# Gated linear attention followed by a rational feed-forward: explicit activation-table loads, the state's decay folded into an exp, and a new order of steps

## The chip, the cores and the metric

The kernel runs on one core of a Trainium2 chip. The metric is the device time in microseconds (us) of one execution; lower is better. Each time given is the median over several executions of the same program. The engines are called PE (matrix products; PEld is its weight load), DVE (vector), ACT (scalar: exp, ln, reciprocal, casts), POOL (GpSimd) and SP (which only issues transfers).

## The reference

Two stages, in float32. The first is a recurrent attention with a forget gate for each key channel, over 4 batches, 8 heads, 768 tokens and head size 48:

```python
f = 1.0 / (1.0 + np.exp(-f_logit))
for t in range(S):
    state = f[:, :, t, :, None] * state + np.einsum('bhd,bhe->bhde', k[:, :, t], v[:, :, t])
    y[:, :, t] = np.einsum('bhd,bhde->bhe', q[:, :, t], state)
```

The second takes the 3072 rows of 384 values that come out of it through a feed-forward of width 2048 with a rational function in the middle:

```python
h = x @ w_in
P = a[0] + a[1] * h + a[2] * h2 + a[3] * h3          # h2 = h*h, h3 = h2*h
Q = 1.0 + np.abs(b[0]) * np.abs(h) + np.abs(b[1]) * h2
out = (P / (Q + 1e-06)) @ w_out
```

## The kernel before

**Units.** The work is cut into 12 units of 256 tokens of one batch: unit n is chunk n // 4 of batch n % 4, so units 0 to 3 have no state to wait for, and unit n needs the state that unit n-4 left. A unit holds two chunks of 128 tokens. All steps of a unit are short functions, and their order, over all units, is written out in the string ORDER (lines 19 to 95): each entry is a step's name, the unit, and its further arguments; `@0` to `@3` names one of four PSUM slots (two banks each) that the step opens. Every engine executes its instructions in exactly that order, so a step that waits holds up all later steps of its engine. Semaphore waits between the engines follow from the data.

**Attention steps of a unit.** `ld` (SP queue for f, k and q, POOL queue for v) loads. `ef` (line 280) is exp(-f), `ls` (line 285) ln(1 + that), both on ACT. `cs` (lines 295 and 300) makes, on PE, the running sums of the logarithms over the tokens with triangular matrices, and with 2 further columns for each pair of heads the sum over a whole chunk, the logarithm of the state's decay. `A` (line 308, ACT) is exp of the running sums, once with scale 1 (x = 1, for k) and once with -1 (x = 0, for q). `ae` (line 444, ACT) is exp of the chunk sums, in two instructions of 64 partitions each, which put the two heads of a pair into the two halves of a small tile whose other halves stay zero. `xa` (line 313, DVE, or POOL with the mark p) multiplies k or q by A. `T` transposes both on PE, `Te` copies them out of PSUM (ACT with the mark s, else DVE), `sc` makes the scores, `mk` (line 358, DVE) masks them, `vm` (POOL) packs v, `yb` and `yi` make the output y, `ic` and `si` the new state, `st` (line 449, DVE) multiplies it by the decay `ae`, and `ye` copies y out of PSUM as x.

**Feed-forward steps.** `h` (line 460) is x @ w_in on PE, four blocks of 128 features in a step; `hy` (line 472) casts them out of PSUM on ACT. The square is `sq` (DVE) or `sa` (line 481, ACT); `ab` is the absolute value (DVE); their sum is `zv` (DVE) or `zd` (line 494, an accumulating transfer issued by POOL). `rq` (line 499) is the reciprocal of the denominator on ACT. The numerator is `p1`, `p2`, `pm` on DVE and a sum by `tv` (line 527, DVE) or `ta` (line 523, an accumulating transfer issued by POOL); `gm` (line 531, DVE) multiplies both. `o` (line 540) is the product with w_out on PE, `oe` (line 548 on ACT with the mark s, else DVE) copies it out, and `so` stores it. Numbers behind a step's unit name the range of 16 feature blocks: `8 16` is a half (2048 elements per partition), `0 16` the whole (4096).

**Activation tables.** ACT evaluates exp, ln and reciprocal from a table set that has to be active. Exp and ln have a common set, reciprocal is in another one. The kernel names the common set once, at its start (line 135); all later loads are placed by the compiler ahead of the instructions that need them. In the trace they stand under the line of the instruction that they serve.

Of the kernel before, what the change touches and what calls it, by code (L numbers as in the profile page):

```python
# [8 lines left out]
F32 = mybir.dt.float32  # L9
BF16 = mybir.dt.bfloat16  # L10
# [12 lines left out]
wi 0 8 16; cz 1; ae 0 2 4; A 0 0 0 2; ls 1; xa 0 0 0 2; xa 0 1 2 4; xa 0 1 0 2; ld 1 q; T 0 2 4 @2; cs 1 @3  # L23
Te 0 2 4 s; fr; ic 0 @1; ae 1; st 0 0; A 1 1; si 0 1; T 0 0 2 @0; xa 1 1 0 4 p; st 0 1; sc 0 1 @2; Te 0 0 2 s
mk 0 1; ld 2 q; A 1 0; wi 2 8 16; ic 1 @1; sc 0 0 @0; ef 3; ld 2 k; wi 1 8 16; st 1 0; fb; ls 2; wi 3 8 16
mk 0 0; ls 3; xa 1 0 0 4 p; cs 2 @3; yb 0 2 4 @2; ae 2; yi 0 1; ld 4 f; vm 1; A 2 0; T 1 @0; wi 2 0 8; A 2 1
yb 0 0 2; wi 3 0 8; Te 1; si 1 1; xa 2 0 0 4 p; ye 0; sc 1 1 @3; sc 1 0 @0; h 0 12 16 @2; mk 1 0; wi 0 0 8
wi 1 0 8; st 1 1; h 0 8 12 @0; ld 2 v; hy 0 12 16; mk 1 1; ld 3 k; yi 1 1 @1; hy 0 8 12; yb 1 0 2; cs 3 @2
xa 2 1; A 3 0; p1 0 8 16; T 2 @3; A 3 1; sq 0 8 16; yb 1 2 4; h 0 4 8 @0; ye 1 s; ab 0 8 16; Te 2 s; pm 0 8 16
h 0 0 4 @1; ld 5 f; ae 3; hy 0 4 8; zv 0 8 16; sc 2 0 @3; hy 0 0 4; h 1 0 4 @2; mk 2 0; ld 3 q; vm 2; ef 4  # L30
ld 3 v; ic 2 @0; p2 0 8 16; hy 1 0 4; h 1 4 8 @1; ld 4 k; sq 0 0 8; ls 4; sc 2 1 @3; hy 1 4 8; h 1 12 16 @2
ab 0 0 8; mk 2 1; xa 3 1 0 4 p; ld 6 f; ef 5; hy 1 12 16; st 2 0; yb 2 2 4 @1; yb 2 0 2; ls 5; xa 3 0; yi 2 1
si 2 1; cs 4 @3; ye 2 s; p1 1 0 8; ld 4 q; sa 1 0 8; h 2 0 4 @2; p1 0 0 8; ab 1 0 8; ld 7 f; T 3 @1; st 2 1
vm 3; ld 4 v; hy 2 0 4; zv 0 0 8; h 1 8 12 @0; ld 5 k; Te 3 s; tv 0 8 16; A 4 1; h 2 4 8 @2; pm 0 0 8; ld 8 f
hy 1 8 12; ic 3 @1; A 4 0; xa 4 1 0 4 p; sc 3 1 @0; st 3 0; ae 4; mk 3 1; ef 6; si 3 1; cs 5 @3; ef 7; st 3 1
xa 4 0 0 4 p; sc 3 0 @0; ld 5 q; hy 2 4 8; h 2 8 12 @1; mk 3 0; ls 6; ld 6 q; ld 5 v; ab 1 8 16; h 2 12 16 @2
ae 5; A 5 0; p1 1 8 16; A 5 1; ld 6 k; yb 3 0 2 @0; p2 1 0 8; hy 2 12 16; yb 3 2 4; p2 0 0 8; yi 3 1; T 4 @3
hy 2 8 12; ye 3; xa 5 0 0 4 p; ls 7; Te 4; ld 7 q; ta 0 0 8; pm 1 0 8; sc 4 0 @2; si 4 0 @1; ic 4; rq 0 0 16
sc 4 1 @0; p1 2 8 16; cs 6 @3; ta 1 0 8; zv 1 0 8; wo 0 4; st 4 0; vm 4; mk 4 1; xa 5 1 0 4 p; si 4 1; st 4 1
h 3 12 16 @0; mk 4 0; vm 5; A 6 1; wo 8 12; si 5 0 @1; gm 0 0 8; ic 5; ae 6; ef 8; wo 12 16; h 3 8 12 @2  # L40
A 6 0; wo 4 8; st 5 0; ab 2 8 16; hy 3 12 16; ld 6 v; yb 4 2 4 @3; sq 1 8 16; yi 4 0; hy 3 8 12; h 3 4 8 @0
xa 6 1; sa 2 8 16; yb 4 0 2; pm 1 8 16; h 3 0 4 @2; ld 7 v; hy 3 4 8; gm 0 8 16; si 5 1; yi 4 1; ls 8; T 5 @0
ab 2 0 8; hy 3 0 4; st 5 1; p1 2 0 8; o 0 1 0 4 @1; Te 5 s; sq 2 0 8; cs 7 @2; ye 4 s; sa 3 0 8; p2 2 8 16
h 4 4 8 @0; p2 1 8 16; xa 6 0; o 0 0 0 4; ae 7; ta 1 8 16; hy 4 4 8; h 4 0 4 @3; zv 1 8 16; zd 2 0 8; A 7 1
sc 5 1 @0; pm 2 0 8; A 7 0; o 0 0 12 16; o 0 1 12 16; mk 5 1; xa 7 0 0 4 p; sc 5 0 @2; o 0 1 4 8; rq 1 0 16
mk 5 0; yb 5 2 4 @0; o 0 0 4 8; ld 10 q; pm 2 8 16; ld 7 k; o 0 1 8 12; o 0 0 8 12; zv 2 8 16; T 6 @2
hy 4 0 4; p1 3 0 8; yi 5 0; yi 5 1; yb 5 0 2; gm 1 0 8; oe 0 0 2 s; h 4 12 16 @3; Te 6 s; so 0 0 2; gm 1 8 16
h 4 8 12 @1; ye 5 s; sq 3 8 16; hy 4 12 16; o 1 0 12 16 @2; ld 9 f; hy 4 8 12; ab 3 0 8; si 6 0 @0; ic 6
tv 2 8 16; sc 6 1 @3; rq 2 0 16; o 1 1 12 16; zd 3 0 8; sc 6 0 @1; ab 3 8 16; o 1 0 0 4; mk 6 1; o 1 0 8 12
xa 7 1 0 4 p; o 1 0 4 8; mk 6 0; o 1 1 0 4; sa 4 0 16; zd 3 8 16; o 1 1 4 8; p2 2 0 8; st 6 0; vm 6; tv 2 0 8  # L50
yb 6 2 4 @3; yb 6 0 2; o 1 1 8 12; p1 3 8 16; ld 9 v; yi 6 1; yi 6 0; gm 2 8 16; h 5 0 4 @1; oe 1 0 2 s
ye 6 s; so 1 0 2; pm 3 0 8; T 7 @2; hy 5 0 4; si 6 1; ld 10 f; p2 3 0 16; h 5 12 16 @3; Te 7 s; ld 8 q
rq 3 0 8; p1 4 0 8; o 2 0 12 16 @1; h 5 4 8 @2; gm 2 0 8; rq 3 8 16; st 6 1; vm 7; o 2 0 8 12; ld 8 v
pm 3 8 16; ld 9 k; cs 8 @0; hy 5 12 16; ab 4 8 16; o 2 1 0 4; ld 11 f; tv 3 0 8; hy 5 4 8; sc 7 1 @3
o 2 1 8 12; p1 4 8 16; o 2 1 12 16; ab 4 0 8; sc 7 0 @2; o 2 1 4 8; A 8 0; pm 4 0 8; o 2 0 4 8; ef 9; ld 8 k
mk 7 1; xa 8 0 0 4 p; o 2 0 0 4; A 8 1; ef 10; mk 7 0; ld 9 q; yi 7 0 @3; ae 8; ta 3 8 16; oe 2 0 2 s
si 7 0 @0; p2 4 0 8; h 6 0 4 @2; sa 5 0 8; p1 5 0 8; yb 7 0 2; pm 4 8 16; ic 7; ls 9; yb 7 2 4; h 5 8 12 @1
p2 4 8 16; hy 6 0 4; st 7 0; ta 4 8 16; ls 10; tv 4 0 8; yi 7 1; si 7 1; h 6 4 8 @2; hy 5 8 12; zd 4 0 8
# [24 lines left out]
o 7 0 12 16; p1 10 0 8; o 7 1 8 12; tv 9 8 16; o 7 0 8 12; sa 10 0 8; yb 11 0 2; gm 8 8 16; h 10 12 16 @2
ye 11 s; pm 9 0 8; o 7 1 12 16; zd 10 0 8; hy 10 12 16; h 11 4 8 @1; pm 10 0 8; ta 9 0 8; hy 10 8 12
# [19 lines left out]
def kernel(  # L104
# [12 lines left out]
    nc = tc.nc  # L117
# [492 lines left out]
```

## Time and profile before

| | |
|---|---|
| median of 3 runs | 237.73 us (235.79 to 239.01) |
| profiled execution, its time | 236.52 us |
| profiled execution, its span on the core | 234.8 us |
| PE busy | 197.0 us, 2868 matrix products |
| DVE busy | 195.4 us |
| ACT busy | 200.4 us, of it 16 table loads |
| POOL busy | 84.3 us |
| read and written in HBM | 25.17 MB and 4.72 MB |

The span is the profiled execution alone, from its first to its last recorded event; the time of that execution is 1.7 us longer. Busy times are unions of an engine's instructions. Three engines are busy for 83 to 85% of the span, so no share by itself says which of them sets the time; that is read stage by stage.

### The profile page before, as it was taken

How to read it: one execution, taken by the hardware profiler on the slowest of the kernel's cores; microseconds unless marked ns; L12 is line 12 of the kernel's file. 1: busy time of each engine (PE TensorE's matmuls, PEld its weight loads, DVE VectorE, ACT ScalarE, POOL GpSimd, SP SyncE). 2: the span in 40 equal slices, each digit the busy share in tenths (PEclk: the TensorE clock that was granted, in tenths of full speed). 3: DMA queues.
4: the chain of work that ended last, by engine and by line, in shares of the span. 5: the costliest groups of instructions: out<-in, count | busy, mean ns of one | idle time of the engine just before them, and what ended most of it. 6: DMA issues, size and time to landing. Idle time of an engine off the chain costs nothing.

```text
span 234.8 us, 6576 instructions
## 1 busy us (share of the span) xinstructions
PE 197.0 (84%) x2868; PEld 140.4 (60%) x2868; DVE 195.4 (83%) x225; ACT 200.4 (85%) x208; POOL 84.3 (36%) x95
## 2 busy tenths in 40 slices
PE   0246998999499789999888399998999999999972
PEld 0234676787357557667466366856766776867540
DVE  3147696999999969999998817999998999999970
ACT  2657347999989999999999999799899999999841
POOL 5207902508584141460341160170746431212000
PEclk9998599999859999999999979999999999999999
DMA  6999999795799986789989994489799999979723
GB/s 145 246 228 259 226 210 204 108 254 127 123 159 147 178 159 159 175 148 219 265 169 198 261 225 40 92 172 178 150 197 199 210 202 190 194 162 207 163 67 67
DMA packets 61388, 41.58 MB, mean 177 GB/s; under 512 B 51376, under 2 KB 56496, under 8 KB 61360
## 3 DMA queue, kind: packets, MB, share of 16 engines
q0 software_dynamic: 20096, 22.29, 58.8%
q1 hardware_dynamic: 40976, 18.88, 34.7%
q8 instruction: 22, 0.36, 0.6%
q14 instruction: 6, 0.05, 0.1%
q10 hardware_dynamic: 288, 0.00, 0.1%
HBM read 25.17 MB, written 4.72 MB: 127 GB/s over the span
## 4 chain that ended last, share of the span: by engine, by line
PE 34%; ACT 29%; DVE 24%; issue 8%; DMA 2%; SPq 1%; DVEq 0%; ACTq 0%
PE hp L460 11%; PE op L540 9%; ACT hy L472 7%; ACT qi L499 5%; DVE scm L358 4%; DVE hy L514 4%; PE y L371 3%; ACT A L308 3%; ACT h L481 3%; DVE g L531 3%; PE cs L295 3%; PE tp L327 3%; DVE g L519 2%; DMA f<-in_f_logit_dram 2%; PE sc L350 2%
## 5 line engine op out<-in xcount | busy, mean ns | idle before, releaser
L460 PE MATMUL hp<-x,w_in_sb 128*128 128x256 bf16 x576 | 70.4, 275 | 6.3 <-ACT ae L444 3.5
L540 PE MATMUL op<-w_out_sb,g 128*128 128x384 bf16 x384 | 70.5, 329 | 2.0 <-DVE g L531 1.8
L460 PEld LDWEIGHTS <-w_in_sb 128*128 128x128 bf16 x576 | 55.3, 98 | 17.9 <-issue 8.7
L472 ACT CAST hy<-hp 128x1024 bf16<-128x1024 f32 x48 | 47.6, 1016 | 7.9 <-PE hp L460 7.6
L540 PEld LDWEIGHTS <-g 128*128 128x128 bf16 x384 | 35.7, 98 | 25.0 <-DVE g L531 2.8
L499 ACT ACTIVATE qi<-z 128x2048 bf16<-128x2048 bf16 (+1 forms) x20 | 45.0, 2258 | 0.1
L494 POOL DMA_DIRECT2D z<-h x17 | 17.6, 1074 | 47.3 <-DVE z L485 15.1
L358 DVE TENSOR_TENSOR scm<-sc,mask 128x1024 bf16<-128x1024 f32 x24 | 28.8, 1218 | 4.6 <-PE sc L350 4.5
L531 DVE TENSOR_TENSOR g<-g,qi 128x2048 bf16<-128x2048 bf16 (+1 forms) x22 | 28.9, 1316 | 0.9 <-ACT qi L499 0.7
L519 DVE TENSOR_TENSOR g<-g,h 128x2048 bf16<-128x2048 bf16 x24 | 29.2, 1225 | 0.0
L481 ACT ACTIVATE h<-hy 128x2048 bf16<-128x2048 bf16 (+1 forms) x13 | 26.5, 2048 | 0.0
L523 POOL DMA_DIRECT2D g<-hy x15 | 13.8, 922 | 31.3 <-DVE hy L514 18.9
L514 DVE TENSOR_SCALAR hy<-hy,a_sb 128x2048 bf16<-128x2048 bf16 (+1 forms) x23 | 22.5, 987 | 0.2
L295 PE MATMUL cs<-lsp,Ui 128*128 128x384 bf16 (+1 forms) x39 | 12.1, 374 | 11.1 <-ACT lsp L285 10.5
L308 ACT ACTIVATE A<-cs 128x768 f32<-128x768 f32 (+1 forms) x26 | 19.1, 763 | 2.2 <-PE cs L300 2.0
L313 POOL TENSOR_TENSOR qkp<-q,A 128x768 bf16<-128x768 f32 x8 | 15.4, 1927 | 15.6 <-ACT A L308 14.0
L449 DVE TENSOR_TENSOR state<-sv,ae 128x384 bf16<-128x384 f32 x20 | 11.0, 551 | 10.2 <-PE sv L426 6.7
L313 POOL TENSOR_TENSOR qkp<-k,A 128x768 bf16<-128x768 f32 x7 | 14.3, 2045 | 14.2 <-ACT A L308 14.2
L509 DVE TENSOR_SCALAR g<-hy,a_sb 128x2048 bf16<-128x2048 bf16 (+1 forms) x21 | 18.5, 883 | 0.5 <-ACT hy L472 0.3
L327 PE MATMUL tp<-ident,qkp 128*128 128x128 bf16 x192 | 14.1, 231 | 5.2 <-DVE qkp L313 4.0
L485 DVE TENSOR_SCALAR z<-hy 128x2048 uint16<-128x2048 uint16 (+1 forms) x22 | 17.4, 792 | 0.2 <-ACT hy L472 0.2
L327 PEld LDWEIGHTS <-qkp 128*128 128x128 bf16 x192 | 12.4, 104 | 6.9 <-DVE qkp L313 4.1
(71 smaller groups left out, 267.2 us busy)
## 6 DMA issues: line engine op xcount, KB each, us to landing
z<-h POOLq DMA_DIRECT2D x17, 512.0 KB, 6.7
g<-hy POOLq DMA_DIRECT2D x15, 512.0 KB, 5.5
f<-in_f_logit_dram SPq DMA_DIRECT2D x11, 384.0 KB, 6.0
k<-in_k_dram SPq DMA_DIRECT2D x11, 384.0 KB, 6.8
q<-in_q_dram SPq DMA_DIRECT2D x11, 384.0 KB, 7.1
out_dram<-osb SPq DMA_DIRECT2D x22, 192.0 KB, 3.8
v<-in_v_dram POOLq DMA_DIRECT2D x12, 192.0 KB, 6.8
w_in_sb<-in_moe_w_in_dram POOLq DMA_DIRECT2D x8, 192.0 KB, 6.9
```

What stands on the lines that cost most here:

```text
L308: nc.scalar.activation(t, src, AF.Exp, scale=1.0 if x else -1.0)
L313: i = (nc.gpsimd if eng == "p" else nc.vector).tensor_mul(s["qk"][:, x, :, hh, 0:D], s["qk"[x]][:, hh].rearrange("p h i d -> p i h d"), s[ ...
L327: nc.tensor.transpose(t[:, x, i, p, :], s["qk"][:, x, i, 2 * p:2 * p + 2, :].rearrange("t h d -> t (h d)"), ident)
L358: return nc.vector.tensor_mul(t, s["sc", g].rearrange("s r a i t -> s (r a) (i t)"), mb)
L460: nc.tensor.matmul(t[:, m - m0, :].rearrange("f (j t) -> f j t", j=UB), w_in_sb[:, kk, m * P:(m + 1) * P], s["x"][:, :, kk, :], start=(kk ...
L472: nc.scalar.copy(fl(big(s, "hy"), m0, m1), fl(s["hp", m0], 0, m1 - m0))
L481: return nc.scalar.activation(fl(big(s, "h2"), m0, m1), fl(big(s, "hy"), m0, m1), AF.Square)
L499: return nc.scalar.add_instruction(mybir.InstActivation(name=nc.get_next_instruction_name(), func=AF.Reciprocal, ins=[nc.scalar.lower_ap(f ...
L514: return nc.vector.tensor_scalar(fl(big(s, "hy"), m0, m1), fl(big(s, "hy"), m0, m1), a_sb[:, 1:2], a_sb[:, 0:1], op0=ALU.mult, op1=ALU.add)
L519: return nc.vector.tensor_mul(fl(big(s, "g"), m0, m1), fl(big(s, "g"), m0, m1), fl(big(s, "h2"), m0, m1))
L531: return nc.vector.tensor_mul(fl(big(s, "g"), m0, m1), fl(big(s, "g"), m0, m1), fl(big(s, "qi"), m0, m1))
L540: nc.tensor.matmul(s["op", g][:, j, 0:DM], big(s, "g")[:, m, C * j:C * j + C], w_out_sb[:, m, :], start=(s["on", j] == 1), stop=(s["on", j ...
```

## The change

Five edits. (1) A new step `tab` puts a table load with a named set into ACT's order: `tab 1` ahead of a run of reciprocals, `tab 0` ahead of a run of exp and ln. (2) The step `ae` and its tiles go. `cs` places the chunk sums as 8 columns behind the first (and second) running sum, 4 columns for each of two pairs of heads in each bank, and adds 1e4 to those of the wrong half with a product of the identity and a constant `hsel`; `A` with x = 0 takes these 8 columns along in the same exp, where exp(-1e4) gives the zeros; `st` reads its decay from the tile of `A`. (3) The tiles of `A` get a second buffer and 16 more columns. (4) ORDER is a new order of all steps. In it reciprocals, and exp and ln, stand in longer runs (seven `tab` steps in all), unit 1's `ld f` stands ahead of unit 0's, and `ef 1`, `ls 1`, `cs 1` and `A 1` ahead of most of unit 0's. (5) In the new ORDER some steps are on another engine or take another width: two `tv` and one `zv` of a half become `ta` and `zd`; one `sq` of a half goes to ACT, where the `sa` steps cover two wholes and eleven halves instead of one and twelve; `ye` of units 0 and 3 and `Te` of units 1 and 4 go to ACT, `ye` of unit 8 and `Te` of units 8, 10 and one half of unit 0 to DVE; the evacuations `oe` of units 0 and 2 and of the last half of unit 11 go to DVE, that of unit 5 to ACT; some `p1` are split into halves and some `p2`, `pm` and `gm` joined to wholes. A step `dm` is defined and not used.

The ACT instructions between the first and the third `tab` in the new order, in the program as built, are: reciprocals, casts and copies behind `tab 1`; then, from the last cast of unit 4 to the first of unit 5, one `ye`, `tab 0`, `ls 7`, `ef 8`, `Te 6`, `ef 9`, `A 7 0`, `ls 8`, `A 7 1`, `ls 9`, a whole `sa 3`, `tab 1`, a whole `rq 2` and one `ye`.

```diff
 ORDER = """
-ab_ b a; ci; ld 0 f 0 2; ld 0 k 2 4; cu 1; ld 0 f 2 4; ld 1 f; cu 0; ld 0 v; ld 2 f; cm; fa; ld 0 q 2 4
-ef 0 2 4; ef 0 0 2; ab_ a a; cz 3; cz 0; ld 0 q 0 2; cz 2; ef 1; ls 0 2 4; ls 0 0 2; ld 0 k 0 2; cs 0 0 2 @0
-cs 0 2 4 @1; ld 1 k; A 0 1 0 2; vm 0; A 0 0 2 4; ld 1 v; ld 3 f; A 0 1 2 4; xa 0 0 2 4; ae 0 0 2; ef 2
...
-mk 0 0; ls 3; xa 1 0 0 4 p; cs 2 @3; yb 0 2 4 @2; ae 2; yi 0 1; ld 4 f; vm 1; A 2 0; T 1 @0; wi 2 0 8; A 2 1
-yb 0 0 2; wi 3 0 8; Te 1; si 1 1; xa 2 0 0 4 p; ye 0; sc 1 1 @3; sc 1 0 @0; h 0 12 16 @2; mk 1 0; wi 0 0 8
...
+ab_ a a; cz 3; cu 0; ld 1 f; ab_ b a; ld 0 f 2 4; cu 1; ci; cm; cz 0; wi 0 8 16; ld 2 f; ld 0 f 0 2
+ld 0 k 0 2; cz 2; ld 0 v; ld 0 k 2 4; fa; ef 0 2 4; ef 1; ld 0 q 0 2; ld 0 q 2 4; cz 1; ls 1; cs 1 @0
+ef 0 0 2; ls 0 2 4; ld 1 k; A 1 0; cs 0 2 4 @1; ef 2; ls 0 0 2; A 1 1; cs 0 0 2 @2; vm 0; ld 3 f; ld 1 v
...
+cs 2 @1; ls 3; xa 1 0 0 4 p; sc 0 0 @3; A 2 0; si 1 1; mk 0 0; A 2 1; ld 2 v; st 1 1; fr; T 1 @3; ld 4 f
+wi 2 0 8; yb 0 0 2; Te 1 s; wi 1 0 8; cs 3 @1; ld 5 f; xa 2 1 0 4 p; ye 0 s; sc 1 1 @2; A 3 0; yi 1 1 @3
+mk 1 1; h 0 8 12 @0; A 3 1; vm 1; wi 0 0 8; xa 2 0; sc 1 0 @2; hy 0 8 12; wi 3 0 8; h 0 12 16 @1; mk 1 0
...
+ld 8 f; ta 1 0 8; tab 1; rq 0 8 16; yi 4 0; tv 0 0 8; yb 4 2 4; si 5 1; h 3 12 16 @1; p2 1 8 16; ld 7 v
...
+o 0 1 4 8; p1 2 8 16; tab 0; ls 7; ic 6; p2 2 0 16; ld 9 q; o 0 1 0 4; ef 8; cs 7 @2; Te 6 s; pm 2 0 16
...
 """
-    ind = consts.tile([P, UB], BF16, name="ind")
+    ind = consts.tile([P, UB, 2], BF16, name="ind")
+    hsel = consts.tile([P, UB, 2, 2], BF16, name="hsel")
-    rings("A", 1, [2, 2, DM], F32)
+    rings("A", 2, [2, 2, DM + 16], F32)
-    rings("ae", 2, [HP, UB, 2], F32)
-            for t in ring["ae"]:
-                nc.vector.memset(t.rearrange("p a j r -> p (a j r)"), 0.0)
+            nc.vector.memset(hsel, 0.0)
+            for r in range(2):
+                nc.vector.memset(hsel[E * r:E * r + E, :, :, 1 - r], 1.0e4)
+    def tab(i):
+        nc.scalar.preload_act_table_set(("natural_log_exp_and_others", "reciprocal_and_small")[i])
@@ def cs
-        s["al", a0] = t[:, 0, 448:448 + UB * (a1 - a0)].rearrange("p (a j) -> p a j", j=UB)
+        w0 = nh * D
+        for i in range(2):
+            nc.tensor.matmul(t[:, i, w0:w0 + 8], ident, hsel.rearrange("p j w r -> p (j w r)"),
+                             start=False, stop=True, skip_group_check=True)
         for a in range(a0, a1):
             for i in range(2):
-                nc.tensor.matmul(s["al", a0][:, a - a0, :], s["ls"][:, i, 2 * a:2 * a + 2, :].rearrange("t h d -> t (h d)"),
+                nc.tensor.matmul(_at(t, [[4, UB], [1, 2]], 512 * ((a - a0) // 2) + w0 + 2 * (a % 2)),
+                                 s["ls"][:, i, 2 * a:2 * a + 2, :].rearrange("t h d -> t (h d)"),
                                  ind, start=False, stop=True, skip_group_check=True)
@@ def A
+        nh = 2 * (a1 - a0)
+        n0, n1 = nh * D, nh * D + (0 if x else 8)
+        o0 = (n1 if a0 else 0)
+        t = ring["A"][n % len(ring["A"])][:, x, :, o0:o0 + n1]
+        s["A", x, a0] = t[:, :, 0:n0].rearrange("p i (h d) -> p i h d", h=nh)
+        if a0 == 0 and not x:
+            s["ae"] = t[:, 0, n0:n0 + 4]
+        nc.scalar.activation(t, s["cs", a0][:, :, 0:n1], AF.Exp, scale=1.0 if x else -1.0)
-    def ae(n, a0=0, a1=HP):
-        for r in range(2):
-            p = slice(64 * r, 64 * r + 64)
-            x = nc.scalar.activation(s["ae"][p, a0:a1, :, r], s["al", a0][p], AF.Exp, scale=-1.0)
@@ def st
-        return nc.vector.tensor_mul(state(s, j + 1).rearrange("p a (r d) -> p a r d", r=2),
-                                    s["sv"][:, j].rearrange("p a (r d) -> p a r d", r=2),
-                                    _at(s["ae"], [[2 * UB, HP], [1, 2], [0, D]], 2 * j))
+        return nc.vector.tensor_mul(
+            state(s, j + 1).rearrange("p (b w) (r d) -> p b (w r) d", b=2, r=2),
+            s["sv"][:, j].rearrange("p (b w) (r d) -> p b (w r) d", b=2, r=2),
+            _at(s["ae"], [[DM + 16 if n else DM // 2 + 8, 2], [1, 4], [0, D]], 4 * j))
```

More of the change, by code (lines that the diff above doesn't have):

```diff
@@ L315, in xa @@
             s["qk"[x]][:, hh].rearrange("p h i d -> p i h d"),
[L316 removed]
+            s["A", x, a0])
         return i
@@ L437, in ye, with dm @@
                                     op0=ALU.mult)
[L439 to L445 removed]
     def st(n, j):
         s = unit(n)
[L449 to L451 removed]
+        return nc.vector.tensor_mul(
+            state(s, j + 1).rearrange("p (b w) (r d) -> p b (w r) d", b=2, r=2),
+            s["sv"][:, j].rearrange("p (b w) (r d) -> p b (w r) d", b=2, r=2),
+            _at(s["ae"], [[DM + 16 if n else DM // 2 + 8, 2], [1, 4], [0, D]], 4 * j))
+    def dm(i, sl):
+        t = slot(sl, [P, 2, 512], F32, "dm")
+        for b in range(2):
+            nc.tensor.matmul(t[:, b, :], Ui, mask.rearrange("p a b t -> p (a b t)").bitcast(BF16), start=True, stop=True)
     def h(n, m0, m1, sl):
```

151 lines of the change are left out of this document (70 added, 81 removed).

## The prediction

> **What bounds the kernel now.** I read the page's first part (busy time of each engine), then the busy time by stretch, then the waits of PE, then the chain of waits, and for prices the instruction groups with shapes kept apart. The page first:
>
> ```profile
> span 234.8 us, 6576 instructions
> PE 197.0 (84%) x2868; PEld 140.4 (60%) x2868; DVE 195.4 (83%) x225; ACT 200.4 (85%) x208; POOL 84.3 (36%) x95
> ```
>
> Three engines share the load within 3%, so no engine can be relieved for long without another taking over. The stretches (columns: length, then busy time of PE, PEld, DVE, ACT, POOL, then granted clock of PE, DMA share, GB/s) show where each has room:
>
> ```profile
> 0.00:30.00 30.00, 13.68 (x246) 10.56 (x247) 13.96 (x38) 14.96 (x29) 15.57 (x28) 0.89 1.14 220
> 30.00:60.00 30.00, 27.75 (x540) 22.36 (x540) 27.36 (x32) 25.68 (x35) 10.76 (x9) 1.00 0.99 185
> 60.00:140.00 80.00, 68.37 (x1005) 47.97 (x1005) 71.86 (x75) 78.45 (x76) 32.14 (x33) 0.94 1.01 183
> 140.00:220.00 80.00, 78.81 (x1033) 55.02 (x1031) 75.01 (x76) 75.59 (x65) 25.88 (x26) 1.00 0.90 170
> 220.00:234.80 14.80, 8.44 (x50) 4.45 (x48) 7.25 (x8) 5.71 (x6) 0.00 (x0) 0.96 0.34 81
> ```
>
> There are three regimes. In the first 30 us nothing is full: a dependent start, PE idle 16.3 us. From 60 to 140 ACT is full (78.45 of 80) while PE idles 11.6 and DVE 8.1 us. From 140 to 220 PE is full (idle 1.2). The last 14.8 us are a drain with 6.4 us idle on PE. So the span is PE's 197.05 busy plus 37.75 idle, and only the idle part can shrink. From 30 to 220 it is 2.25 + 11.63 + 1.19 = 15.1 us, and the waits of PE in that window tell who ended it:
>
> ```profile
> PE hp L460 <- ACT ae L444: 3.5, 1, 3.5
> PE sc L350 <- DVE T L338: 3.1, 1, 3.1
> ...
> PE cs L295 <- ACT hy L472: 0.6, 2, 0.4
> ```
>
> Rows that name ACT as releaser are seven, from this first to this last one, and sum to 8.3 us; the other 6.8 us are DVE's or named to nobody. The largest, 3.5 us, is a feed-forward product that waits for a PSUM slot that `ae` reads last, behind table loads.
>
> **The change part by part.** The ACT groups (busy us, mean ns of one, then idle before):
>
> ```profile
> L481 ACT ACTIVATE h<-hy 128x2048 bf16<-128x2048 bf16 x12 | 22.9, 1914 | 0.0
> L308 ACT ACTIVATE A<-cs 128x768 f32<-128x768 f32 x22 | 17.3, 813 | 1.0 <-PE cs L300 0.8
> L499 ACT ACTIVATE qi<-z 128x4096 bf16<-128x4096 bf16 x4 | 14.5, 3630 | 0.0
> L285 ACT ACTIVATE lsp<-f 128x768 bf16<-128x768 f32 x11 | 9.2, 848 | 0.0
> L280 ACT ACTIVATE f<-f 128x768 f32<-128x768 f32 x11 | 9.2, 843 | 0.7 <-DMA f<-in_f_logit_dram 0.6
> L337 ACT COPY T<-tp 128x1024 f32<-128x1024 f32 x9 | 9.2, 1017 | 0.1
> L434 ACT ACTIVATE x<-y 128x768 bf16<-128x768 f32 x10 | 8.2, 820 | 3.3 <-PE y L371 3.3
> L548 ACT ACTIVATE osb<-op 128x768 f32<-128x768 f32 x10 | 8.2, 816 | 1.1 <-PE op L540 0.9 <-ACT hy L472 0.2
> L499 ACT ACT_TABLE_LOAD x5 | 6.4, 1283 | 0.1
> L444 ACT ACT_TABLE_LOAD x4 | 5.1, 1283 | 0.0
> L285 ACT ACT_TABLE_LOAD x3 | 3.8, 1283 | 0.1
> L444 ACT ACTIVATE ae<-cs 64x8 f32<-64x8 f32 x22 | 3.8, 172 | 2.0 <-PE cs L300 1.9
> L481 ACT ACTIVATE h<-hy 128x4096 bf16<-128x4096 bf16 x1 | 3.7, 3655 | 0.0
> L308 ACT ACT_TABLE_LOAD x2 | 2.6, 1283 | 1.0 <-PE cs L300 1.0
> L308 ACT ACTIVATE A<-cs 128x384 f32<-128x384 f32 x4 | 1.9, 489 | 1.2 <-PE cs L300 1.2
> L135 ACT ACT_TABLE_LOAD x1 | 1.3, 1283 | 0.8 <-PEq L594 0.8
> L280 ACT ACT_TABLE_LOAD x1 | 1.3, 1283 | 0.0
> ```
>
> *Table loads.* 5+4+3+2+1+1 = 16 now. The loads at `ef`, `ls`, `A` and `ae` are 10, more than the 5 at `rq`: the compiler changes sets even between exp and ln, although one set serves both. The program as built has 8, the first one and the seven `tab`. ACT sheds 8 x 1.283 = 10.3 us. That a load takes just its own length shows in the chain of waits:
>
> ```profile
> 75.79 0.90 ACT hy L472
> 76.71 1.28 ACT L285
> 78.00 0.84 ACT lsp L285
> ```
>
> A cast ends at 76.69, the load runs from 76.71, the next instruction starts at 78.00: 1.3 us in all. The Trainium skill's page "ScalarE: Activation LUTs" (What ACT_TABLE_LOAD costs) gives the same 1283 ns but adds a drain of about 1380 ns to each switch; this trace shows no such gap. By that page ACT would shed 8 x 2.66 = 21 us, an estimate, and the sum below would lose its allowance for new waits and end 2.8 us lower.
>
> *The decay.* 26 instructions `ae` go: 22 x 172 ns and four shorter ones, at most 26 x 0.172 = 4.4 us. `A` with x = 0 gets 16 elements more; (813 - 489) / 384 = 0.84 ns for an element, so 13 ns each, under 0.2 us in all. *Other moves on ACT.* One more whole square for one half, +1.7; against that one copy of y more (+0.8) and evacuations and copies of T fewer (about -2). ACT comes to 200.4 - 10.3 - 4.4 + 0.2 + 1.7 - 1.2 = 186.4 us. DVE gives up four instructions on a half (two `tv`, one `zv`, one `sq`); POOL and the DMA engines get the three adds as transfers. I cost these at nothing because no engine's wait names a z or g transfer now. Without that cover the reciprocal or `gm` behind one of them would wait for its landing:
>
> ```profile
> z<-h POOLq DMA_DIRECT2D x17, 512.0 KB, 6.7
> ```
>
> *PE.* 13 calls of `cs` each get two products of 8 columns; the nearest row is that of the chunk sums:
>
> ```profile
> L300 PE MATMUL cs<-ind,lsp 128*128 128x2 bf16 x96 | 4.5, 167 | 0.0
> ```
>
> 4.5 / 96 = 0.047 us each, x 26 = +1.2 us, all on the engine that is full after 140. Upper bound: the time of a big product of `o`, 0.18 by the row below, gives +4.8; lower bound nothing. I take 1.2, since the first row has the same tile and nearly the same width. The chunk sums stay as many products.
>
> ```profile
> L540 PE MATMUL op<-w_out_sb,g 128*128 128x384 bf16 x384 | 70.5, 329 | 2.0 <-DVE g L531 1.8 <-DVE state L449 0.2
> ```
>
> *Second buffer of `A`, and the wait moved.* `st` now waits for `A` with x = 0 instead of `ae`, and `A` of unit n+2 may not overwrite until `st` of unit n has read. Behind such an `A` on ACT stand casts that PE needs. It costs nothing as the new order has both `st` of a unit ahead of the `A` two units on, by a unit's work on DVE; bounds: nothing, to one `A` late, 0.8 us each.
>
> *The start.* Before, unit 0's x is late, on this chain:
>
> ```profile
> 24.86 1.14 DVE scm L358
> 26.05 1.88 PE tp L327 x16
> 28.02 0.95 DVE T L338
> 29.16 1.02 DVE x L436
> 30.22 2.78 PE hp L460 x24
> 33.00 0.84 PE y L371 x44
> ```
>
> After the second mask product, which ends at 26.0, PE transposes unit 1, DVE copies that, and only then x is copied and the first feed-forward product starts, 4.2 us later. In the new order unit 1's f is first on the SP queue and its exps stand ahead of most of unit 0's, so unit 1's transposes should be done before that mask product, and both copies are on ACT. What is left is y (0.84) and the copy to x (0.82): 1.7 us, a gain of 2.5. The mask product itself can move either way. Against it, unit 0's first half of f now lands behind three larger transfers and its exps stand behind unit 1's `ef`, `ls` and `A` (0.84 + 0.85 + 2 x 0.81, 3.3 us); for it, before the change DVE was busy in the first 30 us for only 13.96, so most of the time to 24.86 was waiting, much of it for unit 1's k and q, which now start earlier. On POOL one w_in transfer is moved ahead of the first v, and v is needed only after unit 0's `A`. I take 1.5 us earlier, between 2 later and 3 earlier. Sum for the start: -4.0, between -0.5 and -5.5.
>
> *The middle.* Of the 15.1 us idle on PE the 8.3 that ACT ended go, as ACT has 14 us less to do. What is late next is DVE (6.8 kept) and whatever the new order does. New waits I bound by 0 and by those same 8.3, and take the rate of the stretch from 140 to 220, which held four table loads and the same kinds of work: 1.19 / 80 x 190 us = 2.8.
>
> *The end.* The last `gm`, 16 products, an evacuation and a store are the same: nothing.
>
> Sum on the profiled execution: span 234.8 - 4.0 - 8.3 + 2.8 + 1.2 = 226.5. Its time is 1.7 above its span, 236.52 - 234.8, so 228.2; the median of the runs, 237.73, is 1.2 above that execution, so **229.4 us**.
>
> **Rivals.** *The freed time is not used (no change).* From the last cast of unit 4 to the first of unit 5 ACT now has two copies of y, two loads, three `ls`, two `ef`, two `A`, one `Te`, a whole square and a whole reciprocal: 1.64 + 2.57 + 2.54 + 1.69 + 1.63 + 1.02 + 3.66 + 3.63 = 18.4 us without a cast, so PE gets no PSUM for `h`. It has 64 products of `o` there, at 70.5 / 384 = 0.184 us by its row 11.7 us; the remaining 6.7 must come from attention steps that hang on this very ACT block. If they don't, 229.4 + 6.7 = 236.1. For: PE's longest wait for ACT was in such a block. Against: that block had table loads between its parts, and these are gone.
>
> *PE starves in every such block (slower).* The order has three stretches of exp and ln, each followed by whole or paired reciprocals. If PE lost those 6.7 us in all three, the time is 229.4 + 20.1 = 249.5; the mechanism decides from 4.4 us each, which is 2% above today. For: 3.5 us at one such place already. Against: the second and third stretch have casts among them, and POOL, with 64% idle, prepares k and q from two buffers of `A`.
>
> *The clock comes back too (faster).* From 60 to 140 the granted clock was 0.94, so 80 x 0.06 = 4.8 us of PE's cycles were lost, in the stretch with the 3.5 and 3.1 us idle; it was 1.00 where PE was full. If those gaps go, so does this: 229.4 - 4.8 = 224.6. The Trainium skill's page "TensorE: Matmul & The Clock Gate" (Part 1) has the rule: an idle window of some 3.4 us halves the clock. By that rule the trace agrees, and closing two gaps is enough. I don't count it in the forecast because part of that slow PE time lay beside a full ACT.
>
> That the loads don't go is no rival: the built program lists them.
>
> **How the numbers follow.** Forecast 0.52, clock too 0.17, freed time unused 0.20, starving 0.08, something else 0.03. The ends of the start (+3.5, -1.5) and of the new products take the forecast to 228 and 233; with the clock case's 224.6 less about 2 and the third case's 236.1 plus about 1.4, the range is 222.5 to 237.5, which leaves out the slower case and the tails. Faster by over 2% means under 233.0 and slower over 242.5; the runs shown spread over 1.4%, so 2% is about what can be told from no change. Faster: 0.52 + 0.17 + 0.03 of the third case = 0.72; same 0.18; slower 0.10.
>
> **What would show it.** Right: eight loads of 1.28 us in the ACT groups and ACT near 186; the wait of hp for ACT gone and PE idle from 30 to 220 near 10 instead of 15; the first hp product near 26; PE the busiest engine, near 198. Wrong: a wait of PE of several us in the 18.4 us block, named to `gm`, to `T` or to ACT; waits that name z or g transfers; a first hp product after 30; or a clock below 0.94 again between 60 and 140.

## The result and the profile after

| | before | after |
|---|---|---|
| median | 237.4 us (235.79 to 239.09, 20 runs) | 233.93 us (232.27 to 238.07, 20 runs) |
| profiled execution: time, span | 236.52, 234.8 us | 233.26, 231.6 us |

The ratio after to before is 0.9855, 95% interval 0.9825 to 0.9886: 1.5% faster, 3.4 us, where 8.3 were forecast. Ratios leave disturbed runs out; for that reason the ratio of the sixth experiment below rests on two runs.

The page's first part, after:

```profile
span 231.6 us, 6600 instructions
PE 198.5 (86%) x2894; PEld 142.3 (61%) x2894; DVE 198.0 (86%) x221; ACT 185.8 (80%) x172; POOL 92.3 (40%) x98
```

ACT gave up 14.6 us, as forecast. DVE did not give anything up: 198.0 against 195.4, with four instructions fewer. POOL grew by 8.0. The busy time by stretch, after (length, busy time of PE, PEld, DVE, ACT, POOL, then granted clock of PE, DMA share, GB/s), with two short stretches put between that are used further down:

```profile
0.00:30.00 30.00, 14.20 (x260) 10.53 (x264) 12.14 (x39) 14.85 (x23) 15.41 (x28) 1.00 1.08 218
30.00:60.00 30.00, 29.62 (x591) 23.89 (x587) 28.80 (x34) 27.86 (x32) 10.40 (x12) 1.00 0.99 202
60.00:140.00 80.00, 73.26 (x1070) 53.11 (x1069) 78.61 (x71) 70.87 (x62) 37.79 (x33) 0.96 1.01 190
...
130.00:134.00 4.00, 4.00 (x18) 2.21 (x16) 4.00 (x5) 4.00 (x3) 0.00 (x0) 0.57 1.07 211
140.00:220.00 80.00, 74.59 (x948) 51.08 (x947) 74.09 (x75) 69.79 (x57) 28.73 (x27) 0.96 0.93 180
168.00:172.00 4.00, 4.00 (x40) 2.18 (x30) 4.00 (x5) 0.62 (x1) 0.00 (x0) 0.61 0.58 111
220.00:231.60 11.60, 6.79 (x41) 3.68 (x39) 4.38 (x5) 2.49 (x3) 0.00 (x0) 0.90 0.32 79
```

From 60 to 140 ACT was full (78.45 of 80) before; now DVE is (78.61), and ACT has 9 us of room. From 140 to 220 PE was full before; now it idles 5.4 us there and its clock is down from 1.00 to 0.96. The waits of PE from 30 to 220 us, after (total, times, longest):

```profile
PE y L384 <- DVE scm L371: 6.6, 4, 2.7
PE op L550 <- DVE g L541: 5.1, 3, 2.7
...
PE hp L470 <- ACT A L321: 0.3, 1, 0.3
```

Of the 8.3 us that ACT ended before, 0.3 is left. DVE ends 12.0 (these two rows and one of 0.3) where it ended 5.5. The timeline, after, shows what DVE was doing ahead of both waits of 2.7 us (start, length, instruction, in brackets the idle time before it):

```profile
121.43 1.84 POOL L326 TENSOR_TENSOR qkp<-q,A 128x768 bf16<-128x768 f32 x1
122.34 5.04 DVE L519 TENSOR_SCALAR g<-hy,a_sb 128x2048 bf16<-128x2048 bf16 x1
...
124.34 2.48 POOL L326 TENSOR_TENSOR qkp<-k,A 128x768 bf16<-128x768 f32 x1
...
129.71 1.67 PE L550 MATMUL op<-w_out_sb,g 128*128 128x384 bf16 x6 [2.68 <-DVE g L541]
...
150.25 2.36 DVE L371 TENSOR_TENSOR scm<-sc,mask 128x1024 bf16<-128x1024 f32 x2 [0.21 <-PE sc L363]
150.40 1.81 POOL L326 TENSOR_TENSOR qkp<-q,A 128x768 bf16<-128x768 f32 x1 [4.09 <-ACT A L321]
...
160.28 4.86 DVE L524 TENSOR_SCALAR hy<-hy,a_sb 128x4096 bf16<-128x4096 bf16 x1
161.38 2.66 POOL L326 TENSOR_TENSOR qkp<-q,A 128x768 bf16<-128x768 f32 x1
...
166.32 0.24 PE L384 MATMUL y<-scm,v 64*32 64x128 bf16 x4 [2.70 <-DVE scm L371]
```

Read the first place from the top. A `p1` of a half, which took 0.805 us on average before, starts at 122.34 while POOL multiplies q by A, and ends at 127.38, just behind POOL's next product, which ends at 126.82. Behind it on DVE stand a sum and `gm`, which end at 129.65; PE starts at 129.71, after 2.68 us of nothing. In the second place a whole `p2` (1.34 us elsewhere) takes 4.86 beside another product, and behind it stands the mask product for which PE waits 2.70. I call this a *hold*. The product at 124.34 is k of unit 9, which DVE multiplied before: the list of the change leaves out that this one and q of unit 6 went to POOL, and k of units 4 and 5 to DVE. The stretches above show the clock behind the two waits, in the four us from 130 and from 168: granted 0.57 and 0.61, which is 4 x 0.43 = 1.7 and 4 x 0.39 = 1.6 us of PE's cycles. It fell at two more places of the busy part, behind waits of 1.88 us (ending at 65.42) and 2.21 us (ending at 214.36). The pair of mask products at 150.25 reads PSUM, and ran at its usual 1.2 us each beside a product of POOL.

The groups, after (busy us, mean ns of one, idle before):

```profile
L519 DVE TENSOR_SCALAR g<-hy,a_sb 128x2048 bf16<-128x2048 bf16 x22 | 23.2, 1057 | 0.0
...
L280 ACT ACT_TABLE_LOAD x7 | 9.0, 1283 | 0.1
L524 DVE TENSOR_SCALAR hy<-hy,a_sb 128x4096 bf16<-128x4096 bf16 x3 | 7.5, 2513 | 0.1
```

A `p1` of a half averages 1057 ns where it was 805, a whole `p2` 2513 where it was 1336. With their other two groups `p1` and `p2` come to 49.8 us, for 41.0 before. Summed over all DVE instructions that run over 0.15 us longer than the shortest of their line and shape, the excess is 5.1 us before and 12.4 after.

### The profile page after: what moved, and what is told of

Same layout as the page of the kernel before. It is cut to its first block, busy times and chain, and to the rows that moved or that the text cites. A ratio compares the mean times of both kernels' runs of the same rounds, so it can differ in the third digit from the quotient of the medians.

```text
span 231.6 us, 6600 instructions
## 1 busy us (share of the span) xinstructions
PE 198.5 (86%) x2894; PEld 142.3 (61%) x2894; DVE 198.0 (86%) x221; ACT 185.8 (80%) x172; POOL 92.3 (40%) x98
## 4 chain that ended last, share of the span: by engine, by line
PE 43%; DVE 25%; DMA 12%; issue 10%; ACT 6%; POOL 2%; SPq 1%; DVEq 0%; ACTq 0%; POOLq 0%
PE op L550 18%; PE hp L470 11%; DVE scm L371 5%; DMA out_dram<-osb 5%; DVE g L519 5%; PE y L384 4%; DMA f<-in_f_logit_dram 4%; PE tp L340 4%; DMA g<-hy 3%; DVE g L529 2%; ACT qi L509 2%; DVE z L495 2%; DVE g L541 2%; DVE qkp L326 2%; PE cs L299 2%
## 5 line engine op out<-in xcount | busy, mean ns | idle before, releaser
L470 PE MATMUL hp<-x,w_in_sb 128*128 128x256 bf16 x576 | 68.3, 273 | 0.3 <-ACT A L321 0.3
L533 POOL DMA_DIRECT2D g<-hy x17 | 18.3, 1118 | 43.9 <-DVE g L529 20.1
L504 POOL DMA_DIRECT2D z<-h x18 | 20.8, 1202 | 24.7 <-ACT hy L482 9.8
L529 DVE TENSOR_TENSOR g<-g,h 128x2048 bf16<-128x2048 bf16 (+1 forms) x22 | 28.9, 1323 | 0.0
L519 DVE TENSOR_SCALAR g<-hy,a_sb 128x2048 bf16<-128x2048 bf16 (+1 forms) x23 | 26.4, 1146 | 0.0
L321 ACT ACTIVATE A<-cs 128x784 f32<-128x784 f32 (+3 forms) x26 | 19.4, 780 | 3.2 <-PE cs L307 3.2
L204 POOL DMA_DIRECT2D v<-in_v_dram x12 | 12.2, 1016 | 23.7 <-PE y L384 10.0
L558 ACT ACTIVATE osb<-op 128x768 f32<-128x768 f32 (+1 forms) x10 | 7.8, 782 | 15.8 <-DMA out_dram<-osb 7.9
L384 PE MATMUL y<-scm,v 64*32 64x128 bf16 x384 | 15.4, 227 | 5.1 <-DVE scm L371 5.1
L284 ACT ACTIVATE f<-f 128x768 f32<-128x768 f32 (+1 forms) x13 | 10.4, 805 | 7.4 <-DMA f<-in_f_logit_dram 7.4
## 6 DMA issues: line engine op xcount, KB each, us to landing
out_dram<-osb SPq DMA_DIRECT2D x22, 192.0 KB, 5.1
v<-in_v_dram POOLq DMA_DIRECT2D x12, 192.0 KB, 5.8
w_in_sb<-in_moe_w_in_dram POOLq DMA_DIRECT2D x8, 192.0 KB, 6.7
```

The lines of the kernel that those rows point to most:

```text
L384: nc.tensor.matmul(s["y"][32 * a:32 * a + 32, j, kk * C:kk * C + C].rearrange("e (i t) -> e i t", i=2), lhsT, rhs, start=(j, a) not in s[" ...
L470: nc.tensor.matmul(t[:, m - m0, :].rearrange("f (j t) -> f j t", j=UB), w_in_sb[:, kk, m * P:(m + 1) * P], s["x"][:, :, kk, :], start=(kk ...
L519: return nc.vector.tensor_scalar(fl(big(s, "g"), m0, m1), fl(big(s, "hy"), m0, m1), a_sb[:, 3:4], a_sb[:, 2:3], op0=ALU.mult, op1=ALU.add)
L529: return nc.vector.tensor_mul(fl(big(s, "g"), m0, m1), fl(big(s, "g"), m0, m1), fl(big(s, "h2"), m0, m1))
```

## The experiments

All ratios are to the kernel before, measured beside it on the same chip, with 95% intervals.

**1 to 3: the change in parts, in the old order.** The named loads alone (the step `tab` of the change, nine times, ahead of each run of exp and ln and each run of reciprocals in the old ORDER; the diff shows the first three), the decay columns and second buffers of A alone, and both:

```diff
+tab 1
 rq 0 0 16
...
+tab 0
 A 6 1
...
+tab 1
 rq 1 0 16
...
```

> The kernel before in its own order, with nothing but nine named table loads put ahead of its runs of reciprocals and of exp and ln; 10 loads instead of 16, so ACT sheds 6 x 1.283 = 7.7 us. Theory D (the loads were worth it, and the new order gives part back through DVE and late transfers): PE's waits for ACT go and the ratio to before is 0.975 to 0.985, as good as the whole change. Rival O (the old order can't use the freed time, the gain comes from the new order): ratio 0.993 to 1.0.

> The kernel before in its own order, with the decay as columns of the exp and the second buffer of A, and no named loads: 26 small exps go (4.4 us of ACT), 26 small products come (1.2 us of PE), 15 loads by the compiler. Theory D: a small gain, ratio 0.985 to 0.995, since the largest wait of PE for ACT (3.5 us) hung on the decay's exp. Rival O: 0.995 to 1.003.

> All code edits of the change and nine named loads, but the old order of steps and the old split over the engines. Theory D: ratio 0.965 to 0.98, faster than the whole change (0.9855), DVE's time held up beside POOL stays near 5 us as before, where the change has 12. Rival O: ratio 0.99 to 1.0, and the new order is what gains.

Measured: loads alone 227.52 us, 0.9605 (0.9547 to 0.9662); decay alone 232.16 us, 0.9797 (0.9741 to 0.9853); both 227.67 us, 0.9596 (0.9536 to 0.9656). The page and the stretch from 60 to 140 of the loads alone:

```profile
PE 194.1 (86%) x2868; PEld 139.3 (62%) x2868; DVE 195.7 (87%) x225; ACT 192.3 (85%) x202; POOL 84.7 (38%) x95
```

```profile
60.00:140.00 80.00, 74.21 (x1181) 53.09 (x1179) 78.37 (x82) 77.16 (x75) 32.65 (x34) 0.98 1.04 187
```

Six loads fewer (10 for 16), and 9.7 us less than the kernel before beside it (237.21): the whole forecast gain and more, without the new order. The decay is worth 4.8 us alone and nothing once the loads are named. PE makes the same 2868 products in 194.1 us instead of 197.0, since its clock is up (0.98 from 60 to 140, where it was 0.94): its busy time is not fixed. The new order with the same edits stands at 0.9855, so it gives back some 6 us. All three runs gained more than either of the expected ranges allowed.

**4: a second output buffer in the changed kernel.**

```diff
-    rings("x", 4, [UB, KD, C], BF16)
-    rings("osb", 1, [UB, DM], F32)
+    rings("x", 3, [UB, KD, C], BF16)
+    rings("osb", 2, [UB, DM], F32)
```

> The changed kernel with two buffers for the output tile (and three instead of four for x, for the room). Theory S (the waits of ACT for the stores, 7.9 us in the profile, lie on the path at the end): ratio to before 0.970 to 0.978, 2 to 3 us less than the change, and ACT's waits for stores gone. Rival: the last units are bound by DVE and PE anyway, ratio 0.982 to 0.988.

In the changed kernel the last evacuations wait for the store ahead of them, with nothing of the kind before. ACT's waits, and then the chain of waits near the end, after:

```profile
ACT osb L558 <- DMA out_dram<-osb: 7.9, 3, 3.5
```

```profile
199.91 10.45 DMA out_dram<-osb
...
211.14 1.91 ACT qi L509
213.08 1.24 DVE g L541
214.36 9.65 PE op L550 x48
```

A store takes 10.45 us to land, and on ACT the evacuation that needs its buffer stands ahead of a reciprocal, on which `gm` and the last products hang. The room for the second buffer came from x, which has three buffers here instead of four. Measured: 231.67 us, 0.9749 (0.9696 to 0.9802), the store waits gone, PE's waits for `mk` (6.6 us) and for `gm` (3.5 us) still there. So the one buffer costs about 0.0106 x 237 = 2.5 us, and the larger part of the loss lies elsewhere.

**5: the first loads of the changed kernel in another order** (both halves of unit 0's f ahead of unit 1's; unit 2's f and the first w_in transfer later):

```diff
-ab_ a a; cz 3; cu 0; ld 1 f; ab_ b a; ld 0 f 2 4; cu 1; ci; cm; cz 0; wi 0 8 16; ld 2 f; ld 0 f 0 2
+ab_ b a; cz 3; cu 0; ld 0 f 2 4; ab_ a a; ld 0 f 0 2; cu 1; ci; cm; cz 0; ld 1 f; ld 0 v
...
```

> The changed kernel, in which only the first loads stand in another order: both halves of unit 0's f ahead of unit 1's f, and unit 2's f and the first part of w_in behind unit 0's k and q. Theory L (the start gained nothing because the first half of f landed at 11.6 us): the hole of 2.2 us on ACT before it goes, the first hp product comes at 28 instead of 30.2, and the ratio to before is 0.972 to 0.980, against 0.9855 of the change. Rival: what is gained at the start waits later for DVE, ratio 0.983 to 0.988.

Measured: 234.04 us, 0.99 (0.9822 to 0.9978), not told apart from the changed kernel; the first feed-forward product starts at 29.4 us instead of 30.2. This edit frees none of the lost time.

**6 and 7: the held instructions moved.** In the sixth the steps `p2 1 0 8`, `p1 3 0 16`, `p1 5 8 16` and `p2 7 0 16` were put later on DVE; the seventh joins this to the edits of 4 and 5.

> The changed kernel with four one-input DVE instructions (two p1, two p2) moved a few places later on DVE, from where they ran 1.5 to 4.2 us too long beside POOL's products. Nothing is removed. Theory H (DVE's instructions are held while POOL computes, and that is what the new order lost): the DVE time of p1 and p2 falls by 5 us or more from 49.9, DVE from 198 to about 192, and the ratio is 0.965 to 0.978. Rival W (those instructions were long because DVE was waiting for something else, or DVE is not the bound): DVE's time may fall, the ratio stays 0.982 to 0.988.

> The changed kernel with all three mends: first loads, four moved DVE instructions, two output tiles. If the three losses are separate and are what the new order costs against the old one (e3, 0.9596), the ratio is 0.945 to 0.962. If they overlap, or something else of the order costs the time, it stays at 0.965 to 0.975.

Measured: 0.9637 (0.9558 to 0.9715) and 227.51 us, 0.9628 (0.9553 to 0.9702). But the holds did not go; the timeline of the seventh, at the place of the `p1` above:

```profile
121.58 1.84 POOL L325 TENSOR_TENSOR qkp<-q,A 128x768 bf16<-128x768 f32 x1
122.49 5.57 DVE L536 TENSOR_TENSOR g<-g,hy 128x2048 bf16<-128x2048 bf16 x1
...
124.49 2.48 POOL L325 TENSOR_TENSOR qkp<-k,A 128x768 bf16<-128x768 f32 x1
...
129.25 0.99 PE L549 MATMUL op<-w_out_sb,g 128*128 128x384 bf16 x5 [2.08 <-DVE g L540]
```

Whatever instruction stands there, here the sum `tv`, is held as long: the place is held, not the step. The excess as summed above is still 12.4 us. What the moves changed is who stands behind it: `gm` is one instruction nearer, PE's gap is 2.08 us and not 2.68, and no wait of PE from 30 to 220 is longer than 2.1. In total PE's idle time from 30 to 220 hardly changed (12.3 us for 12.5); its busy time over the whole run fell, from 198.5 to 192.0 us. The three mends together gave no more than the moves alone, so the second output buffer, worth 0.0106 by itself in experiment 4, added nothing here that can be told. The stretch from 60 to 140 of the seventh shows a clock of 1.00, where the changed kernel has 0.96:

```profile
60.00:140.00 80.00, 72.11 (x1098) 52.56 (x1097) 78.64 (x72) 72.83 (x64) 38.27 (x34) 1.00 1.01 193
```

**8: the named loads in the old order, three `p2` moved** (`p2 0 8 16`, `p2 0 0 8` and `p2 6 8 16`, the held ones of experiment 1).

> The old order with named loads (e1, 0.9605), in which three p2 that ran 1.5 us too long beside POOL's products are moved a few places later on DVE. Theory H: ratio 0.945 to 0.956, 1 to 4 us less than e1. Rival W: 0.958 to 0.964.

Measured: 226.41 us, 0.9537 (0.9479 to 0.9595); DVE 192.5 us, the excess 2.6 instead of 6.6. Against experiment 1 the intervals overlap, so the gain of some 1.6 us is not beyond doubt.

**9: the products that hold DVE, taken off POOL.** The changed kernel, with four of its products of k or q on DVE:

```diff
-xa 7 0 0 4 p
+xa 7 0
-xa 9 1 0 4 p
+xa 9 1
-xa 10 0 0 4 p
+xa 10 0
-xa 11 0 0 4 p
+xa 11 0
```

> The changed kernel with four of its 15 products of k or q on GpSimd given back to DVE (q of unit 7, k of unit 9, q of units 10 and 11); nothing else is changed. Two of them close the pairs beside which one DVE instruction took 5.0 and another 4.9 us. Theory 'DVE held beside GpSimd': DVE takes on 4 x 0.95 = 3.8 us and loses the holds beside those products, some 8 of 12.4 us; DVE busy falls from 198 to about 194, the two PE waits of 2.7 us for a mask product and a gm go, and the ratio to the kernel before falls from 0.986 to 0.970 or below. Rival 'the order itself keeps PE waiting for DVE, the holds are only filler': DVE busy rises to 200 or more or the waits move elsewhere, and the ratio stays at 0.98 to 0.99.

Measured: 227.82 us, 0.9584 (0.9532 to 0.9637). The same `p1` in the timeline, then the page and the two groups shown above, of this run:

```profile
121.20 1.85 POOL L324 TENSOR_TENSOR qkp<-q,A 128x768 bf16<-128x768 f32 x1
122.11 1.50 DVE L517 TENSOR_SCALAR g<-hy,a_sb 128x2048 bf16<-128x2048 bf16 x1
122.97 0.91 POOL L531 DMA_DIRECT2D g<-hy  x1
```

```profile
PE 194.8 (86%) x2894; PEld 140.6 (62%) x2894; DVE 193.1 (86%) x225; ACT 185.5 (82%) x172; POOL 84.7 (38%) x94
```

```profile
L517 DVE TENSOR_SCALAR g<-hy,a_sb 128x2048 bf16<-128x2048 bf16 x22 | 19.2, 875 | 0.1
...
L522 DVE TENSOR_SCALAR hy<-hy,a_sb 128x4096 bf16<-128x4096 bf16 x3 | 4.0, 1345 | 0.1
```

The `p1` starts beside the same first product and takes 1.50 us instead of 5.04: it ends 0.56 us behind that product, beside the transfers that POOL issues next. So it was the second product, gone here, that held it for 3.5 us more, and not the issues. DVE took on four products of 0.95 us, 3.8 in all, and its busy time still fell by 4.9, as `p1` and `p2` fell from 49.8 to 40.6. The span is 5.9 us shorter, 3.7 of it PE's busy time at a clock of 0.98 instead of 0.965, and 2.2 its idle time. With these four products moved the new order stands where the old one does (0.9584 and 0.9596). The first theory is borne out, though one late wait of PE for `gm` stays and has grown (3.6 us, 2.2 in the changed kernel). The edit also makes k and q of four units ready at other times; no wait of PE from 30 to 220 us in the changed kernel names a POOL product, which speaks against that as the cause.

**10: the changed kernel without its named loads** (the seven `tab` steps taken out, all else kept).

> The changed kernel without its seven named table loads: the new order, the decay columns and the second buffer of A stay, and the compiler places the loads. It completes the square of named loads (no, yes) by order (old, new): before 1.0, old order with loads and decay 0.960, changed kernel 0.986. Theory 'named loads are worth the same in either order, about 8 us once the decay is folded in': more loads again, and a ratio near 0.986 + 0.02 = 1.005 (old order with decay alone was 0.980, with loads 0.960). Rival 'in the new order ACT isn't the bound any more, DVE is, so that loads are worth little there': a ratio of 0.985 to 0.995. Second rival 'the order is what needs the named loads, since its long runs of one set leave the compiler little to place wrongly': about eight loads, and the ratio of the changed kernel.

Measured: 236.49 us, 0.9898 (0.9847 to 0.9949), with ACT at 195.0 us and 15 loads, these and two single ones:

```profile
L287 ACT ACT_TABLE_LOAD x5 | 6.4, 1283 | 0.1
L507 ACT ACT_TABLE_LOAD x4 | 5.1, 1283 | 0.1
L319 ACT ACT_TABLE_LOAD x4 | 5.1, 1283 | 0.1
```

The seven loads more are 9.2 us on ACT, but naming them moves the time by 0.4% only, and the two intervals overlap. Part of that is chance: without the named loads the holds fall otherwise, and the excess is 8.9 us instead of 12.4. In the old order with the decay it was 2.0% (0.9797 to 0.9596). The ratio is the one that the first rival gave; its reason holds only in part. In this run ACT ended 6.9 us of PE's waits from 30 to 220 and DVE 8.0, where with the named loads it is 0.3 and 12.0: the loads took ACT's waits away, and DVE's grew. The Trainium skill's page "ScalarE activation tables: per-element evaluation and per-set limits" (Table sets in the compiler and the runtime) says that the back end places the loads by the longest run, and breaks ties toward the set of the highest index; no run here shows that rule at work, only what came of it: loads at `ls` (L287) and at `A` (L319), inside runs of exp and ln that one set serves.

**11: experiment 3 with the three moves of experiment 8.**

> The kernel before with named loads, decay columns and second buffers of A in the old order, and three p2 steps moved later on DVE, as in the run of the named loads alone with these moves (ratio 0.954). Theory 'once the loads are named, ACT has room and the decay columns buy nothing': ratio 0.950 to 0.960, ACT 4 us below that run and PE 1 to 3 us above it. Rival 'with DVE relieved of its holds ACT is next, and the 4 us of the decay show': ratio 0.940 or below.

Measured: 228.42 us, 0.9623 (0.9586 to 0.966). Neither theory: no gain at all over experiment 3. Its excess is 6.6 us, for 7.5 in experiment 3: the longest hold of both is a square that takes 3.8 us instead of 1.22, and the moved steps, chosen from the holds of experiment 1, left it where it was. So this run doesn't tell what the decay columns are worth without them.

**12: experiments 4 and 9 together.**

> The changed kernel with both mends that helped it: the four products of k or q back on DVE (alone 0.958) and a second output buffer with x in three buffers (alone 0.975 against the changed kernel's 0.986). Theory 'two separate losses of the new order': they add, 0.958 - 0.011, a ratio of 0.940 to 0.953, about 224.5 us; the waits of the last evacuations for a store (7.9 us in the run of the products alone) go. Rival 'one bound behind both, which the products have already lifted': the ratio stays at 0.955 to 0.962.

Measured: 225.3 us, 0.9451 (0.9392 to 0.951), the fastest kernel of all, faster than the kernel before by 5.5% and than the changed one by 4%. Its page, with a span of 223.0 us:

```profile
PE 194.4 (87%) x2894; PEld 140.0 (63%) x2894; DVE 194.2 (87%) x225; ACT 185.6 (83%) x172; POOL 84.4 (38%) x94
```

The two losses add, 0.9584 - 0.0106 = 0.948, so they are separate. Against experiment 8 (0.9537) the intervals overlap.

## Why the prediction was right in direction and wrong in size

The span is PE's busy and idle time. By its terms, in us (the forecast's columns are worked out from its sum):

| | before | forecast | after |
|---|---|---|---|
| PE busy | 197.05 | 198.25 | 198.47 |
| idle 0 to 30 | 16.32 | 12.3 | 15.80 |
| idle 30 to 220 | 15.07 | 9.6 | 12.53 |
| idle from 220 | 6.36 | 6.36 | 4.81 |
| span | 234.8 | 226.5 | 231.6 |

**Right.** Eight loads of 1283 ns, ACT at 185.8 against 186.4, and PE's waits for ACT from 8.3 to 0.3 us. Experiment 1 shows that this is worth having. `A` with 16 more elements takes 839 ns for 823. No starving in the long block without casts, the slower rival. PE's new products took 2.7 us by their group for the 1.2 of the sum, and PE in all 198.5 for "near 198".

**The step that failed: the new waits, "+2.8".** The prediction named DVE as next, and sized what the new order would make late by the rate of a calm stretch. DVE's own instructions it took at their length from the rows of before, in the words "DVE gives up four instructions", and POOL, "with 64% idle", it counted as cover. The list of the change left out the products that changed sides between DVE and POOL, and no term was there for what a POOL product does to the DVE instruction beside it, although the rows of before held it: `p2` of a half averaged 971 ns over 22 where `p1` of the same shape took 805. The new order put two products close behind one another (at 121.43 and 124.34, and at 157.78 and 161.38) beside DVE instructions ahead of `gm` and `mk`, and the waits named to DVE grew from 5.5 to 12.0 us. In the terms of the sum, PE's idle time from 30 to 220 should have been 6.8 kept and 2.8 new; it was 12.5, so the new waits were 5.7 us. Experiment 9 took four products off POOL, two of them the second ones of these pairs, PE's idle time there came to 10.1 us, and the ratio fell from 0.9855 to 0.9584: 0.027, or 6.4 us, against the 4.5 us by which the result missed the forecast of 229.4. Experiment 7 is nearly as fast (0.9628) with an excess of still 12.4 us, so the sum of the holds is not what counts, but where they fall.

**A premise that failed with it: "only the idle part can shrink".** PE's busy time was 194.1 with the same products in experiment 1. The rival "the clock comes back too" (224.6) is near what the better kernels did: 227.5 us with a mean clock of 0.990 (experiment 1) and 0.999 (7), 225.3 with 0.990 (12), where before had 0.961. In the changed kernel, at 0.965, it did not happen: the old gaps of 3.5 and 3.1 us went, but the clock fell at four places between 30 and 220 us, behind gaps of 1.9, 2.7, 2.7 and 2.2 us. So closing two gaps was not enough, and gaps shorter than the prediction's 3.4 us take the clock down. What these cycles are worth in time was not shown: over the executions of the kernel before that were measured beside the experiments the mean clock lay between 0.953 and 0.981, and the time did not follow it (236.62 us at 0.953, 236.69 at 0.981).

**The start, "-4.0", measured at nothing.** The first hp product starts at 30.17 us (30.22 before). The chain of waits, after, shows why:

```profile
2.49 9.10 DMA f<-in_f_logit_dram
...
19.30 1.82 PE tp L340 x16
...
30.24 1.42 PE hp L470 x12
```

From the first transposes to the first hp it took 10.9 us where it took 15.1, as argued; but the transposes start at 19.3 and not at 15.1. Unit 0's first half of f, behind its other half and the f of units 1 and 2, landed at 11.6 (7.8 before). The prediction named this, and allowed 2 us for all that could make the start later. It brought 0.5 us for the 4.0 of the sum, so over PE's idle time this term is the larger miss, 3.5 us of the 5.1 by which the span was off; but experiment 5 got no time back by another order of these loads, and experiment 9 got more than the miss back with the first hp at 29.4. What an earlier start would be worth was not shown by any run.

**The transfers, "at nothing".** In time this held only in part. ACT's waits for z were 1.8 us after, with none before, and the one output buffer cost 2.5 us, which the prediction's "The end: nothing" passed over: stores landed later (median 3.5 us before, 4.6 after), and the evacuation behind the store at 199.91 had to wait for it. Why they landed later is left open.

**The rival "the freed time is not used" (236.1)** described the outcome better than its reason: the freed time of ACT went unused because of DVE, and not in the 18.4 us block, where PE was busy for 16.8 us.

## What to carry to other kernels

Naming the table set ahead of each run of a function is worth trying by itself first: here it gave 4% in the old order, and the rearrangement made with it gave two thirds of that back. When work is moved, look at which DVE instructions will start beside a GpSimd product and who stands behind them: a product taken off DVE (0.95 us each) added to a hold of 4.2 us. Look at the clock behind each gap of PE too: each of the two drops measured above took 1.6 to 1.7 us of its cycles, though no run shows what they cost in time.

## What the runs showed of the hardware

**A DVE instruction beside a GpSimd product waits for its end, and can be held for a second one.** Where one product had started first, the excess was up to 1.9 us (a half `p2` at 61.93 in the changed kernel took 2.31 us for 0.80, a square at 136.34 in experiment 2 took 3.09 us for 1.22). Where the DVE instruction started ahead of the product it was longer: 2.5 us for a sum at 70.00 in experiment 7, 3.5 for the `p2` at 160.28. Held for two were the `p1` at 122.34 and, in its place, the sum in experiment 7. Also held were a square and a product of k by A on DVE, all with their tensors in SBUF; mask products, which read PSUM, were not. The Trainium skill's page "SBUF — State Buffer" (Who interferes with whom) has the mechanism: VectorE and GpSimd share one pair of SBUF ports, locked for a whole instruction, which a VectorE instruction needs if it runs in a 2-port mode or has two inputs in SBUF. The trace agrees on which kinds are held. By that page the loser is blocked until the other's instruction finishes; here it was blocked past that, from the end of the first product at 123.27 to 126.82, and the `p2` at 160.28 began 1.1 us ahead of the product that held it. Why those products got the ports first is left open; spans on POOL are rough.

**The clock fell behind short gaps of PE, and the length of the gap alone does not say where.** In the changed kernel it fell behind gaps of 1.88, 2.68, 2.70 and 2.21 us. It stayed at 1.00 in the stretch with the gap of 2.08 in experiment 7, and behind one of 2.64 in experiment 5. The shortest of the first and the longest of the second, each with the stretch behind it (the changed kernel, then experiment 5):

```profile
65.42 0.30 PE L384 MATMUL y<-scm,v 64*32 64x128 bf16 x4 [1.88 <-DVE scm L371]
65.00:69.00 4.00, 3.58 (x84) 2.99 (x87) 4.00 (x6) 2.08 (x2) 0.80 (x1) 0.57 1.23 246
...
130.10 2.12 PE L549 MATMUL op<-w_out_sb,g 128*128 128x384 bf16 x12 [2.64 <-DVE g L540]
130.00:134.00 4.00, 3.75 (x26) 2.55 (x27) 4.00 (x5) 4.00 (x3) 0.00 (x0) 1.00 1.06 211
```

The Trainium skill's page "TensorE: Matmul & The Clock Gate" (Part 1) gives some 3.4 us for the window; by these traces a shorter gap can be enough. What decides between two gaps of like length is left open.

**A store took 10.45 us to land** on the chain of the changed kernel, where the median store took 4.6 us. One took 10.2 us before as well, with no evacuation waiting for it.
